# A list scheduler's priorities: from a few load-order constants to a table of 267 numbers, with three PSUM banks for scores

## The chip, the cores and the metric

One NeuronCore of one Trainium2 chip runs the whole program. The metric is the device time of one execution in microseconds (us). TensorE is called PE, VectorE DVE, ScalarE ACT, GpSimd POOL and SyncE SP; SP's queue issues nearly all DMAs.

## What is computed

Agent attention over B = 4 batches of N = 12608 tokens of width C = 128, with 49 agents, followed by one expert layer on the 128 tokens with the highest gate score of each batch. Cut to what matters:

```python
a2k = softmax(scale * agents @ k.T)        # over the 12608 tokens
agent_v = a2k @ v                          # 49 x 128
x = softmax(scale * q @ agents.T) @ agent_v
scores = x @ w_gate
top = argpartition(-scores[b], 128)[:128]  # for each batch b
out = x
out[b, top] += sigmoid(scores[b, top]) * (relu(x[b, top] @ w1) @ w2)   # F = 1024
```

q, k and v are read once (about 26 MB each with padding) and the output is written once.

## The kernel before

**Tiling.** Each batch is 99 columns of 128 tokens, cut into seven chunks (six of 15 columns and one of 9). A full chunk of q, k or v is a load of 0.96 MB into one of six input buffers (ring `inp`). Stores of batches 1, 2 and 3 take their staging tile from the same ring; batch 0's outputs use a ring of two.

**Stages of a batch.** `k_front` (L543) loads a k chunk, computes agent scores on PE in two halves (tiles `S` in PSUM, ring `psS` of SB = 2 banks), and DVE transposes each half into a tile of the ring `sk` and reduces its maximum (`mx`). When all seven k chunks are in, `k_max` (L553) gives the maximum `mb`; `k_exp` (L577) subtracts it on POOL and takes the exponential on ACT. `v_load` and `v_tiles` (L585, L593) accumulate `av` = exp(scores) times v on PE, which frees the `sk` tile; `v_finish` (L607) turns the sum into the weights `ws`. For q, `q_scores` (L653) uses the same `S` banks, DVE, and tiles `sq`; `q_exp`, `q_high`, `q_low` make a pair of float16 numbers (`f`), `q_turn` (L696) transposes them on PE (`fT`) into `ft`. `q_gate` (L720) multiplies each `ft` column with three columns of `ws` into one PSUM bank, `pg`, of the ring `psX`; `q_rates` (L732) makes each token's scale `r` and score `scs` from it, once all seven chunks are there. `q_out` (L751) computes the output (`po` on PE, scaled by DVE, ACT or ACT and POOL into `og`) and stores it. `topk` (L798) finds the ranks of the candidates: PE spreads them into a bank (`all`), DVE and ACT count (`ge`, `ga`), PE sums (`pc`); these banks are of the ring `psR`, which has one. `expert` (L988) gathers 128 rows, computes and scatters them to the output, once for batches 0 to 2 together and once for batch 3.

**The rings that matter here.** `sk` has nine buffers, for k scores (seven tiles a batch), for `ft` of batch 3, and for the first seven eighths of the two expert weight matrices (two buffers, `w1_held` and `w2_held`, `load_weights` L463). PSUM's eight banks are S 2, T 2, O 1, V 1, X 1 and R 1. Outputs of the tail rotate over `OUT_PS` (L541): the O bank and two turns of S.

**What sets the order.** The program is first recorded: each operation (or group of matmuls) has an engine, a price, what it depends on, and the buffers that it takes. `place` (L254) then simulates the engines: whenever one is free it takes, of the operations that are ready and whose buffers are free, the one with the lowest priority number, and the order that results is emitted for each engine. An engine executes its list in order. Priorities come from `load_order` (L367): chunk loads are sorted by `V_AT`, `V_STEP`, `Q_AT`, `Q_STEP`, and everything else is put at an offset from its chunk's place. Tail outputs come last of all:

```python
with rec.at((FILL_AT if (b, c) in filled else end) + n):
    for t0 in range(0, CHUNKS[c], 4):
        q_out(b, c, t0)
```

Batch 0's outputs (`FILL`) get 60 to 66, those of batches 1, 3 and 2 (`TAIL`) `end + n` with `end` = 84, and `load_weights` `end - 5`; a low priority doesn't hold an operation back when nothing else is ready. All recorded calls pass through L1163, so every row of the profile has that line, and rows are told apart by tile names.

Of the kernel before, what the change touches and what calls it, by code (L numbers as in the profile page):

```python
# [24 lines left out]
P = 128  # L25
# [18 lines left out]
TURN_LAG = 1  # L44
GATE_LAG = 2
EXP_LEAD = 2
# [8 lines left out]
FILL_AT = 60  # L55
CHAIN = 30
AV_LAG = 0
WAIT = 0.0
STICK = 0.0
# [17 lines left out]
RATE = {"fp32": 2 / 1.2, "half": 1 / 2.3}  # L77
# [3 lines left out]
class Op:  # L81
    __slots__ = (
        "engine", "calls", "prio", "deps", "cost", "kind", "takes", "uses", "size", "two", "seq", "start", "end", "label",
# [34 lines left out]
class Recorder:  # L118


    def __init__(self, nc):
        self.nc, self.on = nc, True
        self.ops, self.seen, self.rings, self.open = [], {}, {}, None
        self.prio, self.dry = 0.0, False
        for name in ENGINES:
            setattr(self, name, Port(self, name))
# [4 lines left out]
    @contextmanager  # L131
    def at(self, prio):
        old, self.prio = self.prio, prio
        yield
        self.prio = old
# [11 lines left out]
    def add(self, port, method, real, args, kwargs):  # L147
# [9 lines left out]
        if self.open:  # L157
            op = self.open[0]
        else:
            op = Op()  # L160
            op.engine, op.calls, op.prio, op.seq = engine, [], self.prio, len(self.ops)
# [13 lines left out]
    def touch(self, op, ap, write):  # L175
# [18 lines left out]
    def price(self, op, method, outs, ins, kwargs):  # L194
# [9 lines left out]
        two = False  # L204
# [4 lines left out]
        elif op.engine == "PE":  # L209
            weights, moving = (ins[0], ins[1]) if method == "matmul" else (ins[0], ins[0])  # L210
            wide = mybir.dt.size(weights.dtype) == 4
# [3 lines left out]
            load = weights.shape[-1] if method == "matmul" else P  # L215
            if method == "transpose":
                cost = 112 if wide else 56
            elif label.startswith("S_"):
                cost = cols * RATE["fp32"] / 4
            elif label.startswith("av"):  # L220
                cost = 105
            elif wide:
                cost = max(2 * 112 * load / P, cols * RATE["fp32"])
            else:
                cost = max(27, cols * RATE["half"])
            op.kind = label.split("_")[0]
        elif op.engine == "DVE":
            cost = 150 + 1.04 * n
            if method == "reciprocal":
                cost = 150 + 6.3 * n  # L230
            elif method == "transpose":
                cost = 172 + 1.04 * n
            elif method == "memset":
                cost = 60
            elif label.startswith("ft") or label.startswith("idh"):
                cost = 110 + 0.54 * n
            if kwargs.get("accum_out") is not None:
                cost += 82
# [3 lines left out]
        elif op.engine == "ACT":  # L242
            cost = 180 + 0.82 * n
            if label.startswith("s"):
                cost = 190 + 0.9 * n
            if kwargs.get("accum_out") is not None:
                cost += 203
        else:
            cost = 185 + (2.15 if label.startswith("sk") else 1.7) * n if method != "memset" else 100
# [4 lines left out]
def place(rec, wait=0.0, stick=0.0, trace=None):  # L254

    ops = rec.ops
    users, first = {}, {}
    for op in ops:
        for name in op.uses:
            users.setdefault(name, set()).add(op.seq)  # L260
            first.setdefault(name, op.seq)
    for name, seq in first.items():
        ops[seq].takes.append(name)
    room = {}
    for ring, bufs in rec.rings.values():
        room[ring] = bufs
# [3 lines left out]
    for op in ops:  # L270
        for d in op.deps:
            after[d].append(op.seq)
    ready_at = [0.0] * len(ops)
    queue = {e: [] for e in ENGINES.values()}
    for op in ops:
        if not op.deps:
            queue[op.engine].append(op.seq)
    free = {e: 0.0 for e in queue}
    last = {e: None for e in queue}
    events, now, done = [0.0], 0.0, 0  # L280
    ends = []
    dma = 0.0
    order = []
    while done < len(ops):
        if not events:
            stuck = [(ops[x].label, ops[x].kind, ops[x].takes, {rec.rings[t][0]: room[rec.rings[t][0]] for t in ops[x].takes}) for e in queue for x in queue[e]]
            raise RuntimeError(f"stuck at {now}: {stuck[:12]}")
        now = heapq.heappop(events)
        while ends and ends[0][0] <= now + 1e-6:
            _, seq = heapq.heappop(ends)  # L290
            done += 1
            op = ops[seq]
            for x in after[seq]:
                lag = 0.0 if ops[x].engine == op.engine else 60.0
                if op.engine == "PE":
                    lag = 200.0 if ops[x].engine != "PE" else 150.0
                elif op.engine == "ACT" or op.engine == "POOL":
                    lag += 60.0
                if op.engine == "PE" and ops[x].engine == "PE":
                    lag = 0.0  # L300
                ready_at[x] = max(ready_at[x], now + lag)
                missing[x] -= 1
                if not missing[x]:
                    queue[ops[x].engine].append(x)
                    if ready_at[x] > now:
                        heapq.heappush(events, ready_at[x])
# [4 lines left out]
        for e, waiting in queue.items():  # L311
            if free[e] > now + 1e-6:
                continue
            best, soon = None, None
            for x in waiting:
                op = ops[x]
                p = op.prio - (stick if op.kind == last[e] else 0.0)
                key = (p, x)
                if ready_at[x] > now + wait:
# [3 lines left out]
                need = {}  # L323
                for name in op.takes:
                    r = rec.rings[name][0]
                    need[r] = need.get(r, 0) + 1
                if any(room[r] < k for r, k in need.items()):
                    continue
                best = (key, x)
            if best is None:  # L330
                continue
            x = best[1]
            op = ops[x]
            if ready_at[x] > now + 1e-6:
                heapq.heappush(events, ready_at[x])
                continue
            waiting.remove(x)
            for name in op.takes:
                room[rec.rings[name][0]] -= 1
            begin = now  # L340
            if op.two and free["POOL"] > now:
                begin = free["POOL"]
            cost = op.cost
            if e == "PE" and last[e] != op.kind:
                cost += 100.0
            last[e] = op.kind
            op.start = begin
            free[e] = begin + cost
            if op.size:
                if op.kind == "dma_start":  # L350
                    dma = max(dma, begin + 1500.0) + op.size / 420.0
                    end = dma + 400.0
                else:
                    end = free[e] + 2400.0
            else:
                end = free[e]
            op.end = end
            order.append(op)
            heapq.heappush(ends, (end, x))
            heapq.heappush(events, end)  # L360
            if free[e] != end:
                heapq.heappush(events, free[e])
    order.sort(key=lambda op: (op.start, op.seq))
    return order


def load_order(B):  # L367
    at = {}
    for b in range(B):
        for c in range(NCH):  # L370
            at["k", b, c] = NCH * b + c
            at["v", b, c] = V_AT[b] + V_STEP[b] * c + 0.1
            at["q", b, c] = Q_AT[b] + Q_STEP[b] * c + 0.2
    return sorted(at, key=at.get)
# [55 lines left out]
def agent_attention_moe(ctx, tc, qT, kT, va, agT, wgb, w1, w2, consts, qs, outs, capacity):  # L430
    nc = rec = Recorder(tc.nc)
    B = len(outs)
# [18 lines left out]
    psR = rec.pool(ctx.enter_context(tc.tile_pool(name="psR", bufs=1, space=PSUM)), "psR", 1)  # L451
# [89 lines left out]
    OUT_PS = ((psO, "O"), (psS, "S"), (psS, "S"))  # L541
# [11 lines left out]
    def k_max(b):  # L553
# [19 lines left out]
        nc.vector.tensor_copy(mb, pb[:, :A])  # L573
# [122 lines left out]
    def q_turn(b, c, t0):  # L696
# [13 lines left out]
        with rec.group():  # L710
            for t in range(nt):
                nc.tensor.transpose(pt[:2 * A, P * t:P * t + P], f[:, t0 + t, :], idh)
# [85 lines left out]
    def topk(b):  # L798
# [9 lines left out]
        for h in range(2):  # L808
            pool, tag = (psV, "V") if h and b == B - 1 else (psR, "R")
# [19 lines left out]
        pc = psR.tile([P, 512], F32, tag="R", name=f"pc_{b}")  # L829
# [5 lines left out]
        x = t("x", [P, TOP + 2], BF16)  # L835
# [70 lines left out]
    def search(b):  # L906
# [12 lines left out]
        bk = psR.tile([P, 512], F32, tag="R", name=f"bk_{b}")  # L919
# [68 lines left out]
    def expert(group, i, picks, again=False):  # L988
# [4 lines left out]
        pool, ring = (psR, "R") if G == 1 else (psT, "T")  # L993
# [105 lines left out]
    order = load_order(B)  # L1099
    at = {x: i for i, x in enumerate(order)}  # L1100
# [141 lines left out]
```

## Time and profile before

| what | value |
|---|---|
| median of 3 runs | 366.7 us (360.35 to 369.81) |
| the profiled execution | 360.63 us |
| its span, first to last instruction | 358.8 us |
| mean granted TensorE clock | 0.909 |
| bytes moved | 106.69 MB, mean 297 GB/s |

The sum of the prediction is made on the profiled execution: 358.8 us of span and 1.8 us around it. A granted clock of 1.00 is 2.4 GHz, and 0.50 is 1.2 GHz; a number between is a mean over a stretch with both. Matmuls are pipelined, so PE's busy time is longer than the sum of the times at which it takes new work.

### The profile page before, as it was taken

Reading aid. Unit: us, or ns where it says so; the run is one execution under the profiler, and the core shown is the slowest. Engines: PE = TensorE matmul, PEld = TensorE weight load, DVE = VectorE, ACT = ScalarE, POOL = GpSimd, SP = SyncE. Lnnn points to the kernel's source line nnn. Section 1 sums busy time; section 2 is a strip of 40 time slices with the busy share of each in tenths; the row PEclk is TensorE's granted clock in tenths of the full one; section 3 lists DMA queues with packets and bytes.
Section 4 is the critical chain, followed back from the end, with each engine's and each line's share of the span. In section 5 each row is a group of like instructions: output and inputs, shape, how many; then the busy total and the mean of one; then the engine's idle time right before and its main releaser. Section 6 shows DMA issues by size and latency. Waiting matters only on the chain.

```text
span 358.8 us, 8582 instructions
## 1 busy us (share of the span) xinstructions
PE 295.9 (82%) x3524; PEld 190.7 (53%) x3524; DVE 229.0 (64%) x507; ACT 172.8 (48%) x306; POOL 179.7 (50%) x152
## 2 busy tenths in 40 slices
PE   3767688999989779999879999999899498998800
PEld 0112244454655444558535555776597367997700
DVE  0999838778578758692785669646725653765600
ACT  1024344332786625765765466687772451454400
POOL 0046697643783423589231438845531114569641
PEclk9999959999999999998996999899955869999975
DMA  8999969999978999998888899993002023949992
GB/s 303 416 393 418 415 228 331 355 418 325 422 245 307 397 329 395 347 427 344 298 305 248 302 368 420 420 366 111 9 3 111 0 110 126 375 164 414 412 409 105
DMA packets 18203, 106.69 MB, mean 297 GB/s; under 512 B 2032, under 2 KB 3440, under 8 KB 18160
## 3 DMA queue, kind: packets, MB, share of 16 engines
q1 hardware_dynamic: 17472, 105.07, 75.7%
q8 instruction: 30, 0.49, 0.5%
q0 software_dynamic: 256, 0.52, 0.5%
q10 hardware_dynamic: 432, 0.50, 0.4%
q14 instruction: 13, 0.11, 0.1%
HBM read 79.87 MB, written 26.21 MB: 296 GB/s over the span
## 4 chain that ended last, share of the span: by engine, by line
PE 52%; DMA 15%; DVE 15%; POOL 7%; ACT 6%; issue 4%; POOLq 0%; ACTq 0%; DVEq 0%
PE S L1163 17%; PE av L1163 12%; DMA v<-va 8%; PE po L1163 6%; PE fT L1163 6%; DMA out<-og 5%; DVE ge L1163 4%; POOL og L1163 4%; ACT ga L1163 3%; PE ph L1163 3%; DVE sk L1163 2%; PE pg L1163 2%; DMA cst<-consts 2%; DVE sq L1163 2%; DVE qm L1163 2%
## 5 line engine op out<-in xcount | busy, mean ns | idle before, releaser
L1163 PE MATMUL S<-xT,ag_sb 128*32 128x480 f32 (+1 forms) x896 | 108.4, 581 | 20.8 <-DVE mx L1163 6.8
L1163 POOL TENSOR_TENSOR sq<-sq,qm 128x735 f32<-128x735 f32 (+1 forms) x35 | 47.6, 1363 | 85.0 <-DVE qm L1163 70.0
L1163 PEld LDWEIGHTS <-ft 98*128 98x128 f16 x1188 | 60.6, 100 | 27.0 <-issue 25.5
L1163 PE MATMUL av<-v,sk 128*64 128x129 f32 x792 | 59.6, 293 | 8.0 <-DMA v<-va 4.8
L1163 PEld LDWEIGHTS av<-v,sk 128*64 128x64 f32 x792 | 49.9, 145 | 25.2 <-issue 9.7
L1163 PE MATMUL po<-ws,ft 98*128 98x128 f16 x792 | 56.1, 224 | 8.0 <-ACT og L1163 5.4
L1163 ACT COPY ft<-fT 98x896 f16<-98x896 f16 (+2 forms) x49 | 43.4, 898 | 33.3 <-PE fT L1163 33.1
L1163 POOL TENSOR_TENSOR f<-sq,f 128x735 f16<-128x735 f32 (+1 forms) x28 | 41.1, 1469 | 30.6 <-issue 24.0
L1163 PEld LDWEIGHTS S<-xT,ag_sb 128*32 128x32 f32 x896 | 21.8, 111 | 59.7 <-issue 23.0
L1163 POOL TENSOR_TENSOR og<-og,r 128x512 f32<-128x512 f32 (+1 forms) x39 | 35.7, 939 | 32.3 <-ACT og L1163 32.3
L1163 POOL TENSOR_TENSOR sk<-sk,mb 128x735 f32<-128x735 f32 (+1 forms) x28 | 46.8, 1693 | 6.5 <-DVE mb L1163 4.1
L1163 DVE STREAM_TRANSPOSE sq<-S 128x480 f32<-128x480 f32 (+1 forms) x56 | 36.0, 647 | 19.5 <-PE S L1163 17.2
L1163 DVE STREAM_TRANSPOSE sk<-S 128x480 f32<-128x480 f32 (+1 forms) x56 | 35.1, 640 | 20.0 <-PE av L1163 17.0
L1163 ACT ACTIVATE sq<-sq,lift 128x735 f32<-128x735 f32 (+1 forms) x28 | 24.9, 889 | 34.1 <-POOL sq L1163 34.1
L1163 DVE TENSOR_REDUCE mx<-S 128x1 f32<-128x480 f32 (+1 forms) x56 | 33.8, 607 | 4.9 <-PE S L1163 4.5
L1163 PEld LDWEIGHTS <-f 128*98 128x98 f16 x396 | 26.8, 133 | 15.9 <-issue 10.6
L1163 DVE TENSOR_TENSOR og<-po,r 128x512 f32<-128x512 f32 (+1 forms) x42 | 27.0, 660 | 11.8 <-PE po L1163 6.8
L1163 PE MATMUL fT<-idh,f 128*98 128x128 f16 x396 | 31.8, 232 | 1.8 <-POOL f L1163 0.7
L1163 ACT COPY og<-po 128x512 f32<-128x512 f32 (+1 forms) x39 | 20.9, 535 | 24.6 <-PE po L1163 20.0
L1163 DVE TENSOR_REDUCE qm<-sq 128x15 f32<-128x735 f32 (+1 forms) x35 | 30.4, 870 | 2.6 <-ACT sq L1163 1.8
L1163 DVE SCALAR_TENSOR_TENSOR ge<-all,top,minus 128x512 bf16<-128x512 f32 x32 | 24.0, 750 | 12.0 <-ACT ga L1163 8.9
L1163 ACT ACTIVATE ga<-all,top 128x512 bf16<-128x512 f32 x32 | 22.0, 689 | 16.6 <-DVE ge L1163 16.1
(130 smaller groups left out, 244.4 us busy)
## 6 DMA issues: line engine op xcount, KB each, us to landing
v<-va SPq DMA_DIRECT2D x24, 967.5 KB, 7.3
xT<-kT SPq DMA_DIRECT2D x24, 960.0 KB, 7.9
xT<-qT SPq DMA_DIRECT2D x24, 960.0 KB, 7.6
out<-og SPq DMA_DIRECT2D x24, 960.0 KB, 7.2
v<-va SPq DMA_DIRECT2D x4, 580.5 KB, 5.6
xT<-kT SPq DMA_DIRECT2D x4, 576.0 KB, 6.3
xT<-qT SPq DMA_DIRECT2D x4, 576.0 KB, 6.3
out<-og SPq DMA_DIRECT2D x4, 576.0 KB, 8.5
```

The source lines that it names most:

```text
L1163: call(*args, **kwargs)
```

## The change

Priorities become a table, `RANKS`, indexed by step, batch and chunk (`rec.at("k", b, c)` in place of a number); `q_scores`, `q_exp` with `q_high` and `q_low`, `q_turn` and `q_gate` have entries of their own, and so have stores of single chunks. `price` gets new constants, an operation's result is ready `tail` after its engine is free, a matmul group is held `SLACK` = 220.4 ns longer after another engine's result, and an operation of the same kind as the last one on its engine has its number lowered by `STICK` = 75.55. The planner's matmuls cost double while its own model of the clock is low. SB is 3; the ring `psR` is gone, and what used it (`all`, `pc`, the expert of batch 3) takes `psX`, whose single bank the gates hold too; `OUT_PS` has a fourth turn. The first use of an `sk` buffer by anything other than a k score now depends on the first use by all 28 k chunks. The last `fT` group of each `q_turn` of batch 3 depends on `mb` of batch 3. `x` of `topk` has four buffers in place of two. `AV_STEP` is 5 as before. What is computed is the same.

```diff
-SB = 2
-V_AT = (8.5, 15.5, 21.5, 30)
-V_STEP = (0.8, 0.9, 1.0, 0.7)
-Q_AT = (2.5, 11.0, 18.0, 28)
-Q_STEP = (1.1, 1.5, 1.3, 1.2)
...
+SB = 3
...
-FILL_AT = 60
-CHAIN = 30
-AV_LAG = 0
-WAIT = 0.0
-STICK = 0.0
+AV_STEP = 5
+SLACK = 220.4
+STICK = 75.55
...
+        if name in op.uses and not log and self.rings[name][0] == ("skp", "sk"):
+            if name.startswith("sk"):
+                self.keys.append(op.seq)
+            else:
+                op.deps.update(self.keys)
...
-            elif label.startswith("S_"):
-                cost = cols * RATE["fp32"] / 4
-            elif label.startswith("av"):
-                cost = 105
+            elif op.kind == "S":
+                cost = 7.5 + cols / 2.4
+            elif op.kind == "av":
+                cost = 110
...
+class Clock:
+    def __init__(self):
+        self.work, self.until = [], 0.0
+
+    def cost(self, op, t):
...
+        few = op.kind == "pg"
+        c = op.cost * (2.0 if t < self.until and not few else 1.0)
...
+                more = slack if x.engine == "PE" and op.engine != "PE" else 0.0
+                ready[x.seq] = max(ready[x.seq], op.end + lag(op, x) + more)
...
+                key = rank[op.seq]
+                if op.kind == last[e]:
+                    key = (key[0] - stick, key[1])
...
+RANKS = {
+    "setup": 11.4,
+    "k": {
+        0: {0: -654, 1: -654, 2: -576.1, 3: -611.8, 4: -589.3, 5: -462.6, 6: -507.5},
...
+    "v": {
+        0: {0: -652, 1: -148, 2: -606.2, 3: -210.1, 4: -138.8, 5: -111.4, 6: -247},
...
+        3: {0: 166.6, 1: 257.2, 2: 510.5, 3: 569, 4: 881.2, 5: 422, 6: 579.1},
...
+    "rank": {0: -408.8, 1: 398.3, 2: -2.6, 3: 436.6},
+    "weights": {0: 46.5},
...
+    "out": {
+        1: {7: 285.2, 8: 714.3, 9: 801, 10: 530.2, 11: 506.4, 12: 414.5, 13: 448.5},
+        3: {14: 9.7, 15: -550.4, 16: -254, 17: 300.1, 18: -589.5, 19: -120.7, 20: 340.1},
+        2: {21: 26.9, 22: -752.2, 23: -150.8, 24: 583.7, 25: -0.9, 26: -127.4, 27: 68.4},
+    },
+    "expert": {2: 449.8, 3: -591.5},
+}
+def urgency(tag):
+    r = RANKS.get(tag[0], 0.0)
+    for x in tag[1:]:
+        r = r.get(x, 0.0) if isinstance(r, dict) else r
+    return r
...
-    psR = rec.pool(ctx.enter_context(tc.tile_pool(name="psR", bufs=1, space=PSUM)), "psR", 1)
...
-    OUT_PS = ((psO, "O"), (psS, "S"), (psS, "S"))
+    OUT_PS = ((psO, "O"), (psS, "S"), (psS, "S"), (psS, "S"))
...
+        if b == B - 1:
+            turn.deps.add(d["mb_set"].seq)
...
-            pool, tag = (psV, "V") if h and b == B - 1 else (psR, "R")
+            pool, tag = (psV, "V") if h and b == B - 1 else (psX, "X")
...
-        with rec.at((FILL_AT if (b, c) in filled else end) + n):
+        with rec.at("fill" if (b, c) in filled else "out", b, n):
...
-    order = place(rec, WAIT, STICK)
+    order = place(rec, urgency, SLACK, STICK)
```

## Rows read from the trace of the kernel before

**Rows 1.** The page's busy time of each engine, with its share of the span and its number of instructions.

```profile
PE 295.9 (82%) x3524; PEld 190.7 (53%) x3524; DVE 229.0 (64%) x507; ACT 172.8 (48%) x306; POOL 179.7 (50%) x152
```

**Rows 2.** Nine stretches of the span: us from the start, length, busy us of PE, PE's weight loads, DVE, ACT and POOL (with instructions), PE's granted clock, mean busy share of the DMA engines, GB/s.

```profile
0.00:40.00 40.00, 25.16 (x219) 6.78 (x223) 29.10 (x59) 9.56 (x14) 13.23 (x19) 1.00 0.98 386
40.00:60.00 20.00, 14.97 (x140) 8.70 (x136) 11.12 (x18) 8.62 (x11) 16.50 (x11) 0.74 0.78 296
60.00:100.00 40.00, 37.34 (x511) 21.75 (x505) 29.93 (x67) 17.92 (x29) 22.81 (x18) 1.00 0.97 378
100.00:190.00 90.00, 79.48 (x974) 47.12 (x971) 64.54 (x138) 54.58 (x94) 45.07 (x32) 0.97 0.89 336
190.00:250.00 60.00, 59.87 (x755) 37.77 (x753) 40.85 (x94) 37.55 (x65) 33.16 (x24) 0.93 0.90 332
250.00:300.00 50.00, 42.17 (x400) 33.86 (x400) 27.55 (x86) 25.72 (x57) 14.17 (x15) 0.73 0.15 61
300.00:320.00 20.00, 19.00 (x263) 18.00 (x262) 12.63 (x29) 8.12 (x17) 11.71 (x13) 1.00 0.48 189
320.00:341.00 21.00, 17.86 (x290) 16.73 (x287) 12.88 (x21) 10.34 (x20) 17.65 (x21) 1.00 1.01 412
341.00:358.80 17.80, 0.00 (x0) 0.00 (x0) 0.42 (x2) 0.41 (x1) 5.35 (x6) 0.61 0.64 257
```

**Rows 3.** The same view for one stretch of ten us within the sixth.

```profile
260.00:270.00 10.00, 10.00 (x147) 9.80 (x147) 2.92 (x8) 7.32 (x14) 3.65 (x6) 0.50 0.01 2
```

**Rows 4.** SP's queue in order of time, cut: start us, us, the DMA that is issued. The first four are the expert weights, the next the first store, then the last load, then all stores of batches 1, 3 and 2.

```profile
6.60 0.43 SPq L1163 DMA_DIRECT2D w_held<-w  x1
9.34 0.33 SPq L1163 DMA_DIRECT2D w_end<-w  x1
11.89 0.39 SPq L1163 DMA_DIRECT2D w_held<-w  x1
12.32 4.40 SPq L1163 DMA_DIRECT2D w_end<-w  x1
...
115.65 0.35 SPq L1163 DMA_DIRECT2D out<-og  x1
...
240.92 0.33 SPq L1163 DMA_DIRECT2D xT<-qT  x1
270.65 75.47 SPq L1163 DMA_DIRECT2D out<-og  x21
```

**Rows 5.** DVE in order of time around 45 us, cut; at the end of a row, in brackets, the idle time before it and what ended that.

```profile
42.33 1.20 DVE L1163 TENSOR_REDUCE mx<-S 128x1 f32<-128x480 f32 x2
44.69 0.92 DVE L1163 TENSOR_REDUCE qm<-sq 128x15 f32<-128x735 f32 x1 [1.16 <-ACT sq L1163]
46.02 0.25 DVE L1163 RECIPROCAL qm<-qm 128x15 f32<-128x15 f32 x1 [0.41 <-ACT qm L1163]
49.59 1.25 DVE L1163 STREAM_TRANSPOSE sk<-S 128x480 f32<-128x480 f32 x2 [3.32 <-PE av L1163]
```

**Rows 6.** Waits of an engine over the span: who waited for whom, us in total, times, longest.

```profile
DVE sk L1163 <- PE av L1163: 17.0, 8, 4.8
PE S L1163 <- DVE mx L1163: 6.8, 7, 2.4
PE S L1163 <- DVE sk L1163: 2.4, 5, 0.9
PE po L1163 <- ACT og L1163: 5.4, 3, 3.1
PE po L1163 <- DVE og L1163: 2.5, 6, 0.7
SPq L1163 <- PE S L1163: 110.6, 47, 6.0
SPq L1163 <- PE av L1163: 53.2, 23, 6.7
SPq L1163 <- POOL og L1163: 43.8, 20, 8.1
```

**Rows 7.** DVE and PE in order of time, cut: the three rates `r` (batches 1, 2, 3), each the first step after its gates; then the last gates of the span.

```profile
170.21 0.26 DVE L1163 TENSOR_SCALAR r<-pg 128x99 f32<-128x99 f32 x1 [0.50 <-PE pg L1163]
225.81 0.26 DVE L1163 TENSOR_SCALAR r<-pg 128x99 f32<-128x99 f32 x1 [1.17 <-PE pg L1163]
273.67 0.25 DVE L1163 TENSOR_SCALAR r<-pg 128x99 f32<-128x99 f32 x1
263.53 0.98 PE L1163 MATMUL pg<-ws,ft 98*128 98x3 f16 x30
```

**Rows 8.** PE in order of time, cut: for batches 1 and 2 the first `all` and the last `pc` of the ranks, and the first gates of batches 2 and 1.

```profile
160.83 2.55 PE L1163 MATMUL pg<-ws,ft 98*128 98x3 f16 x90
173.14 1.16 PE L1163 MATMUL all<-idf,top 128*128 128x128 f32 x8
196.06 0.18 PE L1163 MATMUL pc<-x,p 128*128 128x10 bf16 x1
222.86 0.95 PE L1163 MATMUL pg<-ws,ft 98*128 98x3 f16 x30
230.18 1.16 PE L1163 MATMUL all<-idf,top 128*128 128x128 f32 x8
254.10 0.18 PE L1163 MATMUL pc<-x,p 128*128 128x10 bf16 x1
```

**Rows 9.** The end of the chain of waits: start us, us, what.

```profile
340.75 4.62 POOL og L1163 x5
345.39 8.37 DMA out<-og
353.82 0.52 issue
354.34 0.50 POOLq L1168
354.84 0.70 POOL out L1163
```

**Rows 10.** The DMA issues of the expert weights: count, KB each, median us from issue to landing.

```profile
w_held<-w SPq DMA_DIRECT2D x2, 448.0 KB, 11.6
w_end<-w SPq DMA_DIRECT2D x2, 64.0 KB, 10.2
```

More of the change, by code (lines that the diff above doesn't have):

```diff
@@ L82 @@
     __slots__ = (
-        "engine", "calls", "prio", "deps", "cost", "kind", "takes", "uses", "size", "two", "seq", "start", "end", "label",
+        "engine", "calls", "tag", "deps", "cost", "kind", "takes", "uses", "size", "two", "tail", "seq", "start", "end", "label",
     )
@@ L209, in price @@
         elif op.engine == "PE":
-            weights, moving = (ins[0], ins[1]) if method == "matmul" else (ins[0], ins[0])
-            wide = mybir.dt.size(weights.dtype) == 4
+            wide = mybir.dt.size(ins[0].dtype) == 4
             cols = 1
@@ L271, in place @@
         for d in op.deps:
[L272 to L288, printed above, removed]
-        while ends and ends[0][0] <= now + 1e-6:
[L290 to L306, printed above, removed]
@@ new lines, in place @@
+            after[d].append(op)
+    ready = [0.0] * len(ops)
+    queue = {e: [op for op in ops if op.engine == e and not op.deps] for e in ENGINES.values()}
+    free = dict.fromkeys(queue, 0.0)
+    last = dict.fromkeys(queue, "")
+    times, ends, order = [0.0], [], []
+    line, clock = 0.0, Clock()
+    while len(order) < len(ops) or ends:
+        if not times:
+            raise RuntimeError("no instruction can begin")
+        now = heapq.heappop(times)
+        while ends and ends[0][0] <= now + 1e-6:
+            op = ops[heapq.heappop(ends)[1]]
+            for x in after[op.seq]:
+                more = slack if x.engine == "PE" and op.engine != "PE" else 0.0
+                ready[x.seq] = max(ready[x.seq], op.end + lag(op, x) + more)
+                missing[x.seq] -= 1
+                if not missing[x.seq]:
+                    queue[x.engine].append(x)
+                    heapq.heappush(times, ready[x.seq])
@@ L313, in place @@
                 continue
[L314 to L319, printed above, removed]
+            best = None
+            for op in waiting:
+                if ready[op.seq] > now + 1e-6:
                     continue
+                key = rank[op.seq]
+                if op.kind == last[e]:
+                    key = (key[0] - stick, key[1])
@@ L321, in place @@
                 if best is not None and key >= best[0]:
                     continue
[L323 to L329, printed above, removed]
+                need = takes[op.seq]
+                if all(room[r] >= need.count(r) for r in need):
+                    best = (key, op)
@@ L330, in place @@
             if best is None:
                 continue
[L332 to L342, printed above, removed]
+            op = best[1]
+            waiting.remove(op)
@@ L343, in place @@
+            order.append(op)
+            for r in takes[op.seq]:
+                room[r] -= 1
+            op.start = max(now, free["POOL"]) if op.two else now
             cost = op.cost
-            if e == "PE" and last[e] != op.kind:
-                cost += 100.0
+            if e == "PE":
+                if last[e] != op.kind:
+                    op.start += AFTER.get(last[e], 50.0)
+                cost = clock.cost(op, op.start)
             last[e] = op.kind
-            op.start = begin
@@ L348, in place @@
[L348 to L374, printed above, removed]
+            free[e] = op.end = op.start + cost
+            if op.kind == "dma_start":
+                line = max(line, op.start + 1600.0) + op.size / 395.0
+                op.end = line + 300.0
+            elif op.size:
+                op.end += 2400.0
@@ new lines, in place @@
+            heapq.heappush(ends, (op.end, op.seq))
+            heapq.heappush(times, op.end)
+            heapq.heappush(times, free[e])
+    return sorted(order, key=lambda op: (op.start, op.seq))
+RANKS = {
+    "setup": 11.4,
[5 rows of a table added]
+    },
+    "kmax": {0: -51.2, 1: -208.6, 2: -323.3, 3: 293.3},
+    "exp": {
[4 rows of a table added]
+    },
[5 rows of a table added]
+    },
[5 rows of a table added]
+    },
+    "fin": {0: -226.7, 1: -86.9, 2: 1.9, 3: -68.6},
[5 rows of a table added]
+    },
[5 rows of a table added]
+    },
+    "turn": {
[4 rows of a table added]
+    },
+    "gate": {
[4 rows of a table added]
+    },
+    "rank": {0: -408.8, 1: 398.3, 2: -2.6, 3: 436.6},
+    "weights": {0: 46.5},
+    "fill": {
+        0: {0: -36.2, 1: -253.5, 2: -41.6, 3: 10.2, 4: -42.1, 5: 308.5, 6: 354.6},
+    },
+    "out": {
[3 rows of a table added]
+    },
+    "expert": {2: 449.8, 3: -591.5},
+}
@@ L1097, in expert @@
         yield
-    order = load_order(B)
-    at = {x: i for i, x in enumerate(order)}
-    end = len(order)
     def run(steps):
@@ L1140, in agent_attention_moe @@
                 topk(b)
-    with rec.at(end - 5):
+    with rec.at("weights", 0):
         load_weights()
     filled.update(FILL)
-    n = 0
-    for b, c in FILL + [(b, c) for b in TAIL for c in range(NCH) if (b, c) not in filled]:
+    for n, (b, c) in enumerate(FILL + [(b, c) for b in TAIL for c in range(NCH) if (b, c) not in filled]):
         if (b, c) not in filled:
             tail.add(b)
-        with rec.at((FILL_AT if (b, c) in filled else end) + n):
+        with rec.at("fill" if (b, c) in filled else "out", b, n):
             for t0 in range(0, CHUNKS[c], 4):
                 q_out(b, c, t0)
-        n += 1
     if fast:
         for group in GROUP:
-            with rec.at(end - CHAIN):
+            with rec.at("expert", group[-1]):
                 run(expert(group, 0, [taken[x] for x in group]))
-    order = place(rec, WAIT, STICK)
+    order = place(rec, urgency, SLACK, STICK)
     rec.on = False
```

124 lines of the change are left out of this document (66 added, 58 removed), and 32 rows, old and new, of the table RANKS.

## The prediction

> **What bounds the kernel now.** I began with the busy shares [rows 1]: PE is the busiest engine with 295.9 of 358.8 us, so 62.9 us of PE idleness are in the span. The table by stretch [rows 2] says where. Idle time of PE is the length less its busy time: 14.8 us in 0 to 40, 5.0 in 40 to 60, 2.7 in 60 to 100, 10.5 in 100 to 190, 0.1 in 190 to 250, 7.8 in 250 to 300, 1.0 in 300 to 320, 3.1 in 320 to 341, and 17.8 after the last matmul. The clock takes a second toll. Where it is granted at 1.2 GHz in place of 2.4, half of the time is lost, which is the length times (1 - granted clock): 5.2 us in 40 to 60, 2.7 in 100 to 190, 4.2 in 190 to 250, 13.5 in 250 to 300, 25.6 in all. PE's work at 2.4 GHz is thus about 295.9 - 25.6 = 270 us. DMA's share is the other bound: 106.69 MB at the 412 GB/s of 320 to 341 are 259 us.
>
> So neither bound is reached, and the same rows show why: they are hit one after the other. From 0 to 40 DMA is full (0.98) while PE idles; from 190 to 250 PE is full (59.87 of 60); from 250 to 300 DMA has a share of 0.15, and PE is there but slow; from 320 DMA is full again while PE runs out of work. SP's queue names the reason [rows 4]: the last load is issued at 240.92, and all 21 stores of batches 1, 3 and 2 lie between 270.65 and 346. Batch 1's rates stood ready at 170.2 and batch 2's at 225.8 [rows 7]: stores waited for their priority, not for data.
>
> The dip at 40 to 60 is another matter. DVE reduced two S halves at 42.33 and could transpose them into `sk` only at 49.59, when PE's `av` had freed a buffer [rows 5]. Both S banks were held meanwhile, so PE had no scores to make and SP no buffer to load into. Over the span DVE waits 17.0 us for `av` in this way, and PE 9.2 us for the two DVE readers of S [rows 6]. Of the nine `sk` buffers two had been taken by expert weights that were loaded at 6.60 and 11.89 [rows 4].
>
> **The change, part by part.**
>
> *Seven `sk` buffers become nine, two S banks three.* Weights may now be loaded only after all k scores are in, so k has two more chunks of room, and a blocked S half leaves another bank. In 40 to 60 the idle 5.0 and the slow 5.2 us hang on this one wait; between 0 and 10.2 I take 8, since the blockage at 42 was by two halves, which is one chunk. After 60 the same kind of waits lie in idle 13.3 and slow 6.9 us up to 250; of these 20.2 I take 5, as part of that idleness is for other reasons and PE is full from 190.
>
> *Stores go between loads.* `out` of batches 3 and 2 get numbers down to -752 and batch 3's v 166 to 881, where all outputs had been last. Stores, and PE's `po` before them, move into 170 to 300 and DMA's hole is filled. The stretch 250 to 300 loses 7.8 idle and 13.5 slow us. In the slowest part PE was busy 10.00 of 10 us at a granted 0.50 [rows 3], with gates, transposes and small expert matmuls: not idleness but what PE ran went with the low clock. Other matmuls among these may lift it, and the new planner charges for a low clock; I take 14 of 21.3 (two thirds, bounds 0 and 21.3).
>
> The Trainium skill (TensorE: Matmul & The Clock Gate, The HAM clock gate) puts a low clock down to an idle stretch of PE, so by it closing the gaps is enough and all 13.5 us go: the sum below would be 326. The busy 10.00 at 0.50 speaks against it.
>
> *The end.* PE ends at 341 and the span 17.8 us later: a POOL scaling until 345.4, the last store 8.37 us, the scatter [rows 9]. The last store is this long because DMA is full. With fewer stores left over, and a fourth bank in turn against the 7.9 us that `po` waits for ACT and DVE [rows 6], I take 6 out of 17.8 + 3.1 + 1.0 = 21.9; a lone chunk's POOL, store and scatter keep the rest. POOL, 17.65 busy of 21 in 320 to 341 [rows 2], is late next.
>
> *Ranks in the gates' bank.* Batch 1's ranks hold a bank from 173.14 to 196.2, 23.1 us, batch 2's 24.1 [rows 8]. The next gates came 26.7 us after the one and 9.3 after the other (263.53 [rows 7]), so at the order of before sharing costs nothing; what covers it is that lag. Taken: 0. Bounds: no gain, and a loss of 23.1 for each of two batches.
>
> *Queues.* A store in SP's queue that isn't ready holds back the loads behind it. Waits of SP for POOL's `og` are 43.8 us in 20 now, the longest 8.1 [rows 6], and harmless, as no load follows; SP waits 163.8 us for PE to free buffers anyway. v chunks 0 and 2 of batch 0 (-652, -606.2) also go ahead of most k chunks (-507 to -589), and sit in two of six buffers until `mb`. A loss of 0 (the planner sees both) to 16 (two of the longest waits); I take 4, nearer the first.
>
> *Weights.* 2 x 448 and 2 x 64 KB [rows 10] leave the first 20 us, when DMA is full: 1.05 MB at 412 GB/s are 2.5 us. I take 2 of 0 to 2.5. They land later where DMA has had room.
>
> *Nothing:* `x` with four buffers, the dependence of batch 3's `fT` on `mb` (its gates began at 263.53 [rows 7], well after `mb`), the new prices as such, which issue nothing.
>
> **Sum.** 8 + 5 + 14 + 6 - 0 - 4 + 2 = 31 us off the span: 358.8 - 31 = 327.8, and with 1.8 around it 329.6, say **330 us**. The profiled execution, 360.63, lies 1.7% under the median of the runs shown; I add nothing for that, and the range takes it in.
>
> **Rivals.**
>
> *Nearly all of it goes.* For it: every hole above is one of order, and PE and DMA are free at different times. What stays is PE's 270 us, 14.8 of the start (DMA full), some 12 of the end, and 5: 302, with the 1.8 304, between 290 and 316. Against it: an order made ahead must hit PE and DMA at the same time throughout. Chance 0.13. The Trainium skill (Perfetto Trace Analysis, Identifying the Most-Contended Engine) says that matmul busy share tells badly how near PE is to its limit, and has the weight loads' share looked at: 53% here [rows 1], by which PE has room, only DMA's 259 us bind, and this case would go below 290. No run here shows it yet; the full PE of 190 to 250 had weight loads for 37.77 of 60 us [rows 2].
>
> *Work only changes places.* PE is full from 190 to 250, so each `po` moved there pushes scores and `av` back by as much, the last loads end later, and only waits go: 8 for the dip, 2 of weights, 3 of the end, 13 in all: 358.8 - 13 + 1.8 = 348, between 339 and 356. For it: PE's 59.87 of 60. Against it: DMA and PE are both slack in 250 to 300. Chance 0.17, two thirds of it beyond the 2% below.
>
> *Slower: gates queue behind ranks.* The table gives the ranks of batches 1 and 3 low urgency (398.3, 436.6). If gates of batches 2 and 3 are wanted before the ranks ahead are done, the bank makes gates, rates, stores one chain. It decides once both holds bite: 23.1 + 24.1 = 47 us against the 31 gained, 358.8 - 31 + 47 + 1.8 = 377. One hold alone gives 353. Against it: the lags of 26.7 and 9.3 us, and the planner has the bank as a ring. Chance 0.09.
>
> *The table does little.* An engine takes anything that is ready whatever its number: the weights, with 79, went at 6.60 [rows 4]. If choices are few, gains and queue costs cancel: 356 to 364. Chance 0.06.
>
> **How the numbers follow.** The forecast has 0.55 and its own range is 316 to 344 (each term at half or at one and a half times). About 2% can be told from no change: below 353 against the profiled execution is faster, above 368 slower. Faster: 0.55 + 0.13 + 0.11 = 0.79; same: 0.06 + 0.06 = 0.12; slower 0.09. A range of 302 to 357 takes in the forecast, over half of the first rival and nearly all of the second, about 8 in 10.
>
> **What would show it.** Right: no DVE wait for `av` near 45 us and a granted clock near 1.00 in 40 to 60; weights issued after the last k chunk; stores of batch 1 before the last load, and DMA above half where it was 0.15; a mean clock above 0.93; less than 15 us after the last matmul. Wrong: `pg` waiting for the ranks' DVE or ACT, SP waiting for `og` with loads behind it, POOL full and PE waiting for it, or PE idle for more than 45 us in all.

## The result and the profile after

The changed kernel takes 326.07 us (median of 4 runs, 323.51 to 328.18) against 365.37 us for the kernel before (4 runs). The ratio is 0.900, with a 95% interval of 0.8865 to 0.9134: faster, by 36.2 us by the ratio. Executions of one kernel scatter, the longer ones at a lower mean clock, and the ratios, and with them all differences that are given "by the ratio", leave out those that are over 1.5% above the shortest of their kernel. The forecast was 330 in a range of 302 to 357, so the time is right; the rows and the experiments below show that its parts are not all right.

| | before | after |
|---|---|---|
| profiled execution, us | 360.63 | 326.07 |
| its span, us | 358.8 | 324.3 |
| PE busy, us | 295.9 | 279.5 |
| PE idle, us | 62.9 | 44.8 |
| mean granted clock | 0.909 | 0.954 |
| from the last matmul to the end, us | 17.8 | 5.2 |

The page's busy times, to be read beside [rows 1]:

```profile
PE 279.5 (86%) x3524; PEld 185.5 (57%) x3524; DVE 222.2 (69%) x507; ACT 168.9 (52%) x306; POOL 179.7 (55%) x152
```

The same stretches as in [rows 2], with the time from 300 in one row (columns as there):

```profile
0.00:40.00 40.00, 26.50 (x237) 8.66 (x237) 29.42 (x61) 11.76 (x20) 16.12 (x22) 0.96 0.95 370
40.00:60.00 20.00, 17.91 (x163) 6.85 (x163) 15.43 (x25) 13.60 (x19) 14.29 (x11) 0.91 0.97 362
60.00:100.00 40.00, 36.36 (x444) 21.57 (x436) 27.55 (x52) 19.31 (x26) 28.64 (x20) 0.96 0.93 354
100.00:190.00 90.00, 85.13 (x1172) 53.53 (x1176) 68.68 (x155) 48.99 (x86) 45.96 (x34) 1.00 1.00 392
190.00:250.00 60.00, 54.06 (x761) 41.15 (x749) 37.23 (x91) 39.77 (x74) 40.30 (x32) 0.94 0.83 311
250.00:300.00 50.00, 42.37 (x632) 39.61 (x633) 35.18 (x103) 31.01 (x76) 26.97 (x30) 0.90 0.65 263
300.00:324.30 24.30, 17.20 (x133) 14.10 (x131) 8.68 (x24) 4.50 (x11) 7.46 (x8) 0.95 0.36 142
```

PE's idle time is the first place to look: 62.9 - 44.8 = 18.1 us are gone. Length times (1 - granted clock), summed over the stretches with matmuls, gives 14.8 us in place of 25.6: another 10.8. The remaining 5.6 of the 34.5 us of span are PE's busy time at 2.4 GHz (279.5 - 14.8 = 264.7 against 270.3), an upper estimate of its work, since busy time includes the ends of pipelined matmuls. DMA is the mirror image: 392 GB/s from 100 to 190 where it was 336, and 263 from 250 to 300 where it was 61.

SP's queue in order of time, cut, beside [rows 4]: the first output of batches 1 to 3, the two held weights, the last loads, the remaining stores.

```profile
200.12 0.34 SPq L1214 DMA_DIRECT2D out<-og  x1
...
211.25 0.33 SPq L1214 DMA_DIRECT2D w_held<-w  x1
...
224.28 0.39 SPq L1214 DMA_DIRECT2D w_held<-w  x1
...
235.38 0.80 SPq L1214 DMA_DIRECT2D v<-va  x2
247.01 64.30 SPq L1214 DMA_DIRECT2D out<-og  x18
```

Some stores now go before the last loads, and the weights wait for the k chunks. But of the 21 stores of these batches 18 still come after the last load, and the loads end only some five us earlier. What moved more is that the stores begin 12 us, not 30 us, behind the last load.

PE's waits over the span, and then one of DVE's, beside [rows 6]; the two waits of PE for DVE's readers of S fall from 9.2 to 1.2 us, DVE's wait for `av` from 17.0 to 9.6:

```profile
PE S L1214 <- DVE sk L1214: 0.7, 3, 0.3
...
PE S L1214 <- DVE mx L1214: 0.5, 1, 0.5
```

```profile
DVE sk L1214 <- PE av L1214: 9.6, 7, 2.4
```

### The profile page after: what moved, and what is told of

Its sections match the earlier page's. It is cut to its first block, busy times and chain, and to the rows that moved or that the text cites. A ratio compares the mean times of both kernels' runs of the same rounds, so it can differ in the third digit from the quotient of the medians.

```text
span 324.3 us, 8565 instructions
## 1 busy us (share of the span) xinstructions
PE 279.5 (86%) x3524; PEld 185.5 (57%) x3524; DVE 222.2 (69%) x507; ACT 168.9 (52%) x306; POOL 179.7 (55%) x152
## 4 chain that ended last, share of the span: by engine, by line
PE 51%; DMA 19%; DVE 13%; ACT 10%; issue 4%; POOL 2%; ACTq 0%; POOLq 0%; DVEq 0%
PE S L1214 18%; PE av L1214 12%; DMA v<-va 8%; PE po L1214 8%; ACT ga L1214 5%; PE fT L1214 5%; DMA xT<-qT 4%; DMA xq<-q,idx 4%; DVE ge L1214 4%; DMA cst<-consts 2%; PE py L1214 2%; PE all L1214 2%; DVE qm L1214 2%; PE ph L1214 2%; ACT ft L1214 2%
## 5 line engine op out<-in xcount | busy, mean ns | idle before, releaser
L1214 PE MATMUL S<-xT,ag_sb 128*32 128x480 f32 (+1 forms) x896 | 103.6, 575 | 17.6 <-DMA ag_sb<-agT 6.1
L1214 PEld LDWEIGHTS <-ft 98*128 98x128 f16 x1188 | 59.7, 99 | 19.7 <-issue 18.3
L1214 PE MATMUL av<-v,sk 128*64 128x129 f32 x792 | 54.5, 287 | 5.4 <-DMA v<-va 5.1
L1214 PEld LDWEIGHTS S<-xT,ag_sb 128*32 128x32 f32 x896 | 23.7, 111 | 56.7 <-issue 22.9
L1214 PEld LDWEIGHTS av<-v,sk 128*64 128x64 f32 x792 | 48.3, 143 | 11.8 <-DMA v<-va 6.5
L1214 DVE STREAM_TRANSPOSE sk<-S 128x480 f32<-128x480 f32 (+1 forms) x56 | 34.3, 633 | 9.9 <-PE av L1214 9.6
L1214 PEld LDWEIGHTS <-f 128*98 128x98 f16 x396 | 25.9, 127 | 24.3 <-issue 17.8
L1214 ACT CAST f<-sq 128x735 f16<-128x735 f32 (+1 forms) x28 | 22.1, 789 | 18.3 <-PE fT L1214 13.6
```

The source lines that it names most:

```text
L1214: call(*args, **kwargs)
```

## The experiments

Where a run is compared with the kernel before, that was run on the same chip beside it: medians 363.9 us (the sk rule, all resources, old priorities, outputs last), 363.1 (banks, SLACK 240.4 with the table, the table without the clock charge, experts) and 362.0 (the rest). The means that the ratios go by are 359.1, 359.7 and 362.2. The changed kernel was not run again beside these runs, so differences from its 326.1 us are between sets of runs.

### The sk rule alone

```diff
+        if name in op.uses and not log and self.rings[name][0] == ("skp", "sk"):
+            if name.startswith("sk"):
+                self.keys.append(op.seq)
+            else:
+                op.deps.update(self.keys)
```

> The kernel before, with one thing of the change: nothing but k scores may take an sk buffer until all 28 k chunks have theirs, so the expert weights no longer sit in two of nine. If the two buffers made the dip at 40 to 60 us, as the prediction has it, DVE no longer waits for av near 45 us, the clock of 40 to 60 is near 1.00, and the time is 8 to 13 us under that of the kernel before (ratio 0.965 to 0.98). If the dip is of the old order and only one of its places, DVE waits for av later by as much and the ratio is 0.99 to 1.01.

Measured: 354.6 us (350.6 to 358.4), ratio 0.984 (0.961 to 1.007): 5.8 us by the ratio, less than the 8 to 13 that were expected. The interval takes in no change, so the size is not sure; the trace is clearer. DVE's wait for `av` is gone from the list. Two rows of the table by stretch:

```profile
40.00:60.00 20.00, 15.96 (x178) 7.80 (x180) 15.81 (x28) 9.22 (x13) 17.72 (x12) 1.00 0.85 294
...
250.00:300.00 50.00, 39.22 (x470) 32.73 (x467) 26.77 (x70) 24.54 (x54) 17.08 (x18) 0.91 0.20 81
```

In 40 to 60 the clock is full where it was 0.74 [rows 2], and DVE is busy 15.8 us instead of 11.1; PE still idles for 4.0 us. The hole of 250 to 300 stays (DMA share 0.20). So the mechanism of the dip was the one in the prediction.

### The banks alone

```diff
-SB = 2
+SB = 3
...
-    psR = rec.pool(ctx.enter_context(tc.tile_pool(name="psR", bufs=1, space=PSUM)), "psR", 1)
...
-    OUT_PS = ((psO, "O"), (psS, "S"), (psS, "S"))
+    OUT_PS = ((psO, "O"), (psS, "S"), (psS, "S"), (psS, "S"))
```

(The ranks go to `psX`, and `x` has four buffers, as in the change.)

> The kernel before with the change's PSUM banks alone (three for scores, four turns for outputs, the ranks in the gates' bank), weights in sk buffers from the start as before. The pair of b_keys (ratio 0.984) and b_resources (0.946): if banks and sk buffers add up, this one gives 0.946 / 0.984 = 0.96, about 14 us less than before. If a third bank is of use only when sk has room (both are held by the same blocked transpose), 0.98 to 1.0 and DVE's wait for av stays above 14 us. If the bank is all, 0.94 to 0.95.

Measured: 351.5 us (347.8 to 355.2) against 363.1 (357.3 to 369.4). By the means that a ratio goes by, 350.3 against 359.7, it is 9.4 us less, with no interval taken. DVE's wait for `av` is under the 14 us that were named, so the banks are of use without room in `sk`; which of the parts of this edit does it wasn't tested.

```profile
40.00:60.00 20.00, 15.99 (x163) 7.86 (x163) 13.99 (x26) 10.24 (x14) 18.40 (x12) 0.91 0.90 326
```

```profile
DVE sk L1167 <- PE av L1167: 9.7, 10, 4.0
```

### All resources, old planner and priorities

The two edits above together.

> The kernel before, its planner, prices and priorities, with all of the change's resources: the rule for sk, three banks for scores, four turns of output banks, the ranks in the gates' bank, four buffers for x. If the freed waits of S and sk are worth what the prediction takes for them (8 + 5 + 2 us, and some of the output bank's), the ratio is 0.955 to 0.97, and DMA's hole at 250 to 300 us stays (share under 0.3). If the resources carry most of the change, 0.92 to 0.94. If the shared bank costs where the order doesn't know of it, at or over 1.00, with pg waiting behind pc.

Measured: 339.6 us (338.3 to 341.4), ratio 0.946 (0.934 to 0.959): 19.3 us by the ratio, 15 to 24 by its interval, and between the first two expectations. The two halves add up to 15.2 (5.8 + 9.4), within that scatter. Rows by stretch:

```profile
40.00:60.00 20.00, 17.62 (x212) 9.67 (x204) 17.30 (x31) 11.05 (x15) 19.14 (x13) 1.00 0.96 358
60.00:100.00 40.00, 39.16 (x491) 22.11 (x489) 29.28 (x67) 19.54 (x31) 28.91 (x21) 0.96 0.95 384
100.00:190.00 90.00, 89.18 (x1109) 52.93 (x1106) 70.40 (x159) 56.70 (x97) 44.45 (x32) 0.98 0.97 370
190.00:250.00 60.00, 52.22 (x681) 38.32 (x678) 35.23 (x89) 37.92 (x67) 30.43 (x21) 0.89 0.66 254
250.00:300.00 50.00, 41.79 (x529) 37.74 (x527) 29.32 (x77) 26.73 (x61) 22.17 (x26) 0.86 0.40 164
```

PE is busy for 89.18 of the 90 us from 100 to 190 (79.48 before) and for 52.22 of 60 from 190 to 250 (59.87 before): it is no longer behind there, and it waits. Even the hole is half filled without a word on stores: the outputs that come last start sooner, the last load going at 235.30 in place of 240.92. By the ratios, resources carry 19.3 of the 36.2 us of the change.

### New planner and prices, old priorities

```diff
+def urgency(tag):
+    step, b = tag[0], tag[1]
...
+    if step in ("k", "v", "q"):
+        return PLACE[tag]
...
+    if step == "out":
+        return 84 + tag[2]
-STICK = 75.55
+STICK = 0.0
```

> The changed kernel, with its planner, prices and resources, but the priorities of the kernel before (load order and offsets, outputs of batches 1, 3 and 2 after all else; STICK 0). If the table's order is what fills DMA's hole, the stores stay late, the hole stays, and the time lies 15 to 22 us above the changed kernel (341 to 348). If the prices and resources carry the change, it lies within 6 us of the changed kernel (under 332).

Measured: 337.5 us (336.8 to 340.8), ratio 0.942 (0.928 to 0.956): 2.1 us from the last run, and between the two expectations. Prices and planner with these priorities are worth nothing that can be told. The table is worth the rest: 11.4 us by the two times, some 15 by the two ratios (0.942 and 0.900). The last load is issued at 236.23, the stores begin at 257.04, and DMA's share from 250 to 300 is 0.47, so the hole is smaller than before without the table.

### Outputs last, the rest of the table kept

```diff
+    if tag[0] == "out":
+        return 2000.0 + tag[-1]
     r = RANKS.get(tag[0], 0.0)
```

> The changed kernel with one thing of the old order: outputs of batches 1, 3 and 2 get the numbers 2014 to 2034, after everything else. If stores among the loads are worth the 14 + 6 us that the prediction takes for them, less 4 for the queue, the time lies 12 to 20 us above the changed kernel (338 to 346) and DMA's share in 250 to 300 falls under 0.4. If the table's other numbers carry the gain and stores only change places, it lies within 5 us (under 331).

Measured: 351.3 us (347.7 to 353.8), some 25 us above the changed kernel and 13 above the old priorities, which have outputs last too. SP's queue and a stretch:

```profile
261.19 75.36 SPq L1216 DMA_DIRECT2D out<-og  x20
```

```profile
250.00:300.00 50.00, 41.10 (x532) 37.98 (x529) 32.05 (x99) 31.08 (x75) 21.69 (x24) 0.80 0.43 173
```

Stores are late, DMA's share is 0.43 in place of 0.65, near the 0.4 that was named, and the clock of the stretch is 0.80 where it was 0.90, but more was lost than stores can cost. The table without its own stores is worse than the old order without them. It isn't a measure of the stores: the next but one experiment moves the table's time as far with no store changed.

### Early outputs in the old priorities

```diff
     if step == "out":
-        return 84 + tag[2]
+        return 7 + tag[2]
```

> The kernel of a_old_ranks (new planner and resources, old priorities, 337.5 us), with one number changed: outputs of batches 1, 3 and 2 get 14 to 34 in place of 91 to 111, ahead of most loads. If stores among the loads are what the table is worth, this comes to the changed kernel's 326 within 4 us, with DMA over 0.6 in 250 to 300. If early outputs only push scores and av back, since PE is full, it stays within 3 us of 337.5 or above it.

Measured: 388.6 us (387.5 to 393.0), ratio 1.073 (1.069 to 1.077), 51 us above the same kernel with late outputs. DVE in order of time, cut, the idle time and its cause in brackets:

```profile
193.18 1.29 DVE L1191 TENSOR_TENSOR og<-po,r 128x512 f32<-128x512 f32 x2 [6.60 <-DMA out<-og]
...
199.50 1.29 DVE L1191 TENSOR_TENSOR og<-po,r 128x512 f32<-128x512 f32 x2 [5.04 <-DMA out<-og]
...
205.82 1.29 DVE L1191 TENSOR_TENSOR og<-po,r 128x512 f32<-128x512 f32 x2 [5.02 <-DMA out<-og]
...
212.13 1.29 DVE L1191 TENSOR_TENSOR og<-po,r 128x512 f32<-128x512 f32 x2 [5.03 <-DMA out<-og]
```

Each output waits for the store before it to give back its staging tile, and DVE's whole queue stands behind it: five stores went one at a time, with no load among them, and the last load was issued at 301.98. The clock is 0.72 from 190 to 250. This is the rival "work only changes places" and worse; stores ahead of loads are not a gain in themselves. A milder shift of the outputs wasn't tried.

### Small shifts: SLACK by 20 ns

```diff
-SLACK = 220.4
+SLACK = 240.4
```

and 200.4 in the other run with the table.

> The changed kernel with SLACK 240.4 in place of 220.4, and nothing else: the planner's other choices follow from 20 ns. If the table's 11 us over the old priorities are a property of its numbers, the time stays within 4 us of the changed kernel. If the numbers are fitted to the one order that this planner makes of them, and any shift of a price makes another order, it lies 5 to 15 us above, like the old priorities (331 to 341).

> The changed kernel with SLACK 200.4, the shift of the jitter run the other way. If the table is fitted to one order, 331 to 345. If 220.4 only was too near to a bad neighbour, within 4 us of 326.

> The kernel of a_old_ranks with SLACK 240.4 in place of 220.4: the same 20 ns that cost the table 12 us. If the table is fitted to one order, and load order and offsets are not, this lies within 4 us of 337.5. If any order of this planner scatters by that much, it lies 5 us or more away, up or down.

Measured with the table: 338.1 us (335.5 to 340.7) at 240.4, and 365.1 us (362.5 to 366.8; ratio 1.008, 1.003 to 1.013) at 200.4. With the old priorities: 338.4 us (338.2 to 343.2), 0.9 from its neighbour. A step of 20 ns in one of the planner's constants takes the table's whole gain or, in the other direction, the whole change's; the run at 200.4 missed both of its expectations, 20 us to the slow side. With load order and offsets the step up does nothing that can be told; the step down wasn't tried there. In the 200.4 run PE's waits begin with

```profile
PE av L1214 <- DMA v<-va: 12.2, 6, 5.4
PE fT L1214 <- POOL f L1214: 9.7, 2, 6.8
```

and 60 to 100 us has PE busy 30.91 of 40: PE stands for loads of v and for POOL's `f`, as if loads came in an order that the engines' lists don't match. That is a reading of the waits; the orders were not compared.

### No charge for a low clock

```diff
-        c = op.cost * (2.0 if t < self.until and not few else 1.0)
+        c = op.cost * 1.0
```

> The changed kernel with the planner's matmuls at one price whatever its model of the clock says. If charging for a low clock is what keeps the granted clock up (0.954 against 0.909), the clock falls to 0.93 or less and the time rises by 5 us or more. If the clock follows from the work's mix and the filled gaps alone, clock and time stay within 0.01 and 4 us, or shift as the jitter run does.

> The kernel of a_old_ranks with the planner's matmuls at one price whatever its clock model says: with the table this made 376 us. If the planner's clock is worth something by itself, the time is 345 us or more and the granted clock below 0.925. If it was the table that fell apart there, 333 to 342 and a clock within 0.01 of 0.936.

Measured with the table: 375.8 us (372.9 to 377.0), above the kernel before; the clock is 0.892. With the old priorities: 324.95 us (324.3 to 326.6), ratio 0.898 (0.895 to 0.901), 12.5 us under the same kernel with the charge, at a clock of 0.941. Both expectations of the second run missed, on the better side. Waits of the table's run from 190 us (DVE to 260, PE to the end):

```profile
DVE og L1214 <- DMA out<-og: 12.1, 2, 10.6
```

```profile
PE S L1214 <- DVE og L1214: 8.3, 1, 8.3
PE pg L1214 <- ACT ga L1214: 6.6, 1, 6.6
```

DVE stands for 10.6 us at an output whose staging tile is still being stored, PE's scores 8.3 us behind it, and gates wait for the ranks in their bank: the slower rival's very row, in an order where the bank bites. The old priorities without the charge, by stretch, and their last load with what follows:

```profile
100.00:190.00 90.00, 88.30 (x1104) 53.38 (x1103) 66.30 (x155) 55.86 (x93) 45.10 (x33) 0.98 0.94 355
190.00:250.00 60.00, 56.48 (x776) 42.35 (x774) 38.80 (x99) 42.00 (x78) 34.47 (x26) 0.93 0.65 257
250.00:300.00 50.00, 46.30 (x560) 42.07 (x559) 30.27 (x73) 24.99 (x56) 27.65 (x30) 0.84 0.62 253
```

```profile
220.93 0.33 SPq L1191 DMA_DIRECT2D xT<-qT  x1
221.57 38.05 SPq L1191 DMA_DIRECT2D out<-og  x4
```

With the charge PE was busy 81.71 us from 100 to 190 and the last load went at 236.23. Here it is 88.30 and 220.93. So the charge isn't what keeps the clock up: without it the old priorities have 0.941, with it 0.936. The same time as the changed kernel's is reached the other way round: no stores of batches 1 to 3 among the loads, but all loads earlier. What the charge itself does to the order, and why that costs 12.5 us, wasn't taken apart.

### Experts early

```diff
-    "expert": {2: 449.8, 3: -591.5},
+    "expert": {2: -1000, 3: -1000},
```

> The changed kernel with both experts' numbers at -1000 (449.8 and -591.5 before). The trace ends with experts on PE, 303 to 319 us, and the last store left at 311. If the three-batch expert is late only by its number, it is done before batch 3's and the time falls by 4 to 8 us. If its PE work only displaces outputs of the tail, 0, within 2 us. If the order as a whole is upset, as a_outs_last, 5 us or more above.

Measured: 335.6 us (332.8 to 338.2), some 9 above the changed kernel: the order as a whole was upset. The three-batch expert is done with `py` at 303 us in place of 319, but the clock of 250 to 300 falls to 0.83 and DMA's share there from 0.65 to 0.49, and the chain ends with the expert of batch 3 all the same.

## Why the prediction was right, and where it was not

**What bounded the kernel** was read rightly. PE and DMA were hit one after the other, and all of the 34.5 us came out of PE's idle time, its low clock, and a little of its busy time; PE has 3524 instructions in both.

**The dip at 40 to 60** was read rightly: weights in two `sk` buffers, both S banks held by one blocked transpose. PE's idle and slow time there was 10.2 us; it is 4.0 with the sk rule, 5.8 with the banks, 2.4 with both, and 3.9 in the changed kernel, where the clock is 0.91 and not near 1.00.

**The sum came near in part by luck.** Its terms were taken by stretch, so they can be set beside the tables. PE's idle and slow time fell by 6.3 us in 40 to 60 (8 taken), by 0.6 between 60 and 250 (5 taken), by 8.7 in 250 to 300 (14 taken) and by 13.6 after 300 (6 taken), and it rose by 0.3 before 40 (2 taken for the weights). Another 5.6 came from PE's busy time, for which nothing was taken, and the 4 lost to the queue have no stretch of their own. So 31 is near the measured 34.5 because the end gave twice what was taken and made up for the others.

**The resources were about the right size, but not in the right place.** "Seven `sk` buffers become nine, two S banks three" had 8 + 5 us and the weights 2, 15 in all; the run with these resources alone gives 19.3, or 15 to 24. The dip's 8 is there: 7.8 us of idle and slow time are gone in 40 to 60. The 5 between 60 and 250 are not: 100 to 190 loses 10.6 us, and 190 to 250 gains 10.1, so that 19.4 of the 20.2 remain. Instead 250 to 300 loses 6.1 us, though nothing in this run was aimed at it. It seems that PE was full from 190 in the kernel before because it had fallen behind earlier; no run tests that by itself.

**The order was about the right size, with its mechanism only half right.** "Stores go between loads" and "the end", less the queue, had 14 + 6 - 4 = 16 us; the table over old priorities is worth 11.4 by times and some 15 by ratios. But only 3 of 21 stores go before the last load, early stores by hand cost 51 us, and the old priorities without the clock charge reach 325 with no store of the tail among the loads. So there is more than one order that gets there. What such orders have in common isn't shown: the run with all resources has PE and DMA full from 100 to 190 too (89.18 of 90, share 0.97), and it takes 339.6.

**"The new prices as such" were put at nothing because they issue nothing, and that reason failed.** With the old priorities, all prices and the new planner together are worth 2.1 us, near nothing. But one line of the price is worth 12.5 us there, and with the table 50 the other way. A price issues no instruction, but it picks the order; it has to be treated like a change of the order.

**The clock.** In 250 to 300 PE idles for 7.6 us after as for 7.8 before, and the granted clock rose from 0.73 to 0.90. The prediction argued from the busy 10.00 of 10 at 0.50 [rows 3] that idleness was not the reason. Stretches of 2 us show more. Before, both falls to 0.50 in 250 to 300 came behind idle time: PE was busy for 2.4 of 4 us from 256 to 260, and the clock was low until 276; it was busy for 0.00 of 2 from 282, and the clock was low until 293. After, there is one such fall: 0.96 of 4 from 270 to 274, and low until 280. So the same idle time went with one low stretch in place of two. The clock also fell with no idle time in PE's row, behind the 99 gates from 222.86 to 225.77; and it fell behind the 90 at 160.83 [rows 8]. The kernel before, in stretches of 2 us:

```profile
222.00:224.00 2.00, 2.00 (x48) 1.21 (x49) 1.85 (x4) 1.21 (x2) 2.00 (x2) 1.00 1.02 416
224.00:226.00 2.00, 2.00 (x71) 1.98 (x69) 0.83 (x2) 1.79 (x4) 2.00 (x2) 0.87 1.02 426
226.00:228.00 2.00, 2.00 (x20) 1.71 (x16) 1.80 (x8) 1.49 (x3) 2.00 (x3) 0.50 1.04 428
...
282.00:284.00 2.00, 0.00 (x0) 0.00 (x0) 1.86 (x5) 1.20 (x4) 0.00 (x0) 0.87 0.00 0
284.00:286.00 2.00, 1.01 (x8) 0.74 (x7) 1.18 (x4) 1.42 (x5) 1.04 (x1) 0.50 0.00 0
```

So both idleness and what PE runs go with a low clock in this kernel. How much of the 16 us from 260 each made isn't separated: it began behind idle time, and gates ran in its middle. The rule that the prediction weighed, of the Trainium skill (TensorE: Matmul & The Clock Gate, The HAM clock gate), is that a low clock follows an idle stretch. The rows from 282 agree with it, and those from 222 do not.

**Ranks in the gates' bank** cost no wait in the order that was shipped, as forecast: PE's waits have none of `pg` for the ranks, though the lags of 26.7 and 9.3 us are gone. PE in order of time, cut, for batches 1 and 2 the last `pc` and the gates behind it, beside [rows 8], and POOL's last step of `ws`, which the gates need too:

```profile
227.85 0.18 PE L1214 MATMUL pc<-x,p 128*128 128x10 bf16 x1
...
230.42 1.74 PE L1214 MATMUL pg<-ws,ft 98*128 98x3 f16 x60
...
266.55 0.17 PE L1214 MATMUL pc<-x,p 128*128 128x10 bf16 x1
...
267.55 2.96 PE L1214 MATMUL pg<-ws,ft 98*128 98x3 f16 x99
```

```profile
228.14 0.19 POOL L1214 TENSOR_TENSOR ws<-g,ws 98x1 f16<-98x1 f32 x1 [0.62 <-DMA w_held<-w]
...
265.84 0.19 POOL L1214 TENSOR_TENSOR ws<-g,ws 98x1 f16<-98x1 f32 x1
```

The gates come 2.6 and 1.0 us behind the ranks, but their weights were ready only at 228.3 and 266.0. The bank and the weights come free together, so there is no lag left to cover a delay. A bank of their own for the ranks in this order wasn't tried: the eight banks are taken.

**The end** had 6 us of 21.9 and gave 13.6: 5.2 us follow the last matmul in place of 17.8. The last store is issued at 311, and the span ends with experts:

```profile
297.31 5.76 DMA xq<-q,idx
...
312.86 1.79 PE py L1214 x16
314.65 0.89 PE ph L1214 x8
315.54 3.59 PE py L1214 x32
319.16 0.36 DVE ey L1214
```

Against [rows 9] the bound there is no longer POOL and a store but a gather, PE and a scatter. POOL was named as late next, and wasn't.

**The rivals.** "Nearly all of it goes" did not come: 45 us of PE idleness remain. The Trainium skill (Perfetto Trace Analysis, Identifying the Most-Contended Engine) has PE's room judged by the share of its peak that it reaches and by the weight loads' busy share, and not by the busy share of matmuls. The time below 290 that the prediction drew from this did not come either, though weight loads took only 53.53 of the 90 us from 100 to 190, where the matmul row was within 5 us of full. "The table does little" was given 0.06 and names something real: over half of the gain (19.3 of 36.2) came without table and new planner, and all of it with the old priorities, the new planner and no clock charge.

## What to carry to other kernels

When a change brings resources and an order together, run the resources under the old order first: here they were over half of the gain. The sk rule alone was worth about what the stretch of the blocked banks lost by it (5.8 and 6.2 us); with the banks more was gained, most of it in other stretches. And an order from a table that was fitted to one planner is one point: shift a price by 20 ns and see whether the gain is still there before counting on it.

## What was not expected of the hardware

One blocked transpose goes with a low clock as well as a wait: PE was busy for 0.70 of 4 us from 42 to 46, and the clock stood at 0.50 from 46 to 54. With two `sk` buffers freed the granted clock of 40 to 60 us went from 0.74 to 1.00, although PE's idle time there fell only from 5.0 to 4.0 us. The clock also fell with PE's row busy throughout, behind 99 gates; behind another 99, from 199.77 us of the old priorities without the charge, it stayed at 1.00. In-order queues set the size of the bad cases: a single output that waited 10.6 us for its staging tile's store held PE's scores for 8.3 us.
